# The low half of the transposed queries: from VectorE's subtraction to TensorE and a cast on ScalarE

## The chip, the core and the metric

The kernel runs on one core of one Trainium2 chip. A core has five engines, each with its own queue that it works off in order: TensorE (PE, with its weight loads shown apart as PEld), VectorE (DVE), ScalarE (ACT), GpSimd (POOL) and SyncE (SP, which here issues the DMAs). They work out of SBUF; PE writes its products to PSUM. The metric is the device time of one execution in microseconds (us), the median of several runs. Beside it stands one execution that the hardware profiler recorded; all rows of the trace come from that one.

## The reference

Two blocks are applied in turn, twice: four residual steps on an x of 2048 rows by 640 columns.

```
x = x + fourier(layernorm(x));  x = x + attention(layernorm(x))     # layer 0
x = x + fourier(layernorm(x));  x = x + attention(layernorm(x))     # layer 1

attention: 32 heads of 20;  q, k, v = x @ wqkv;  pq, pk = phi(q), phi(k)
  phi(t) = where(t > 0, t + 1, exp(t)) + 1e-6
  kv = sum over rows of pk * v;  z = sum over rows of pk
  o  = (pq @ kv) / (pq @ z + 1e-6);  result o @ wo
```

The attention is linear: keys and values are first summed over all rows, and then each row's queries are multiplied with that sum. So it needs two passes over the rows.

## The kernel before, in words

The rows lie in 16 tiles of 128. Products that need more precision than one pass of TensorE in its reduced format (fp32r) are made of **splits**: a matrix is cast to fp32r, the high half, and what is left over, the low half, is the matrix minus that cast. A product is then high x high, high x low and low x high, all summed in PSUM (`product`, L158 to L169). Of a 128 x 640 tile times a 640 x 640 matrix that makes 5 chunks x 3 x 2 halves of the columns, 30 matmuls of 320 columns. `split` (L132 to L134) makes the cast on ACT (L133) and the subtraction on DVE or POOL (L134).

A layer runs so. The Fourier block is computed on folded rows: sums and differences of mirrored rows and columns (class `Fold`), then matrices of the transform (class `Fourier`, L875 and L918). The attention's first pass (`keys_values`) takes every tile, keeps the queries phi(q) in SBUF (PQ) and sums keys and values (L237). `combine` (L345) multiplies this with the output weights, so that one 640 x 640 matrix M is left. The **second pass** (`outputs`, L448) is what the change is about. For each of 16 tiles, step n does this:

- POOL multiplies the queries of tile n+3 with the key sums (`weigh`, L417).
- PE transposes the weighted queries of tile n+1 into PSUM (`transposed`, L136 to L142), five transposes of 128 x 128.
- `weighted` (L420 to L446) makes the weights of tile n+2 on DVE: it sums each head (L430, to 32 columns), adds 1e-6 (L431), takes the reciprocal (L432) and multiplies the queries with it (L434, L440).
- PE multiplies the split queries of tile n with M: 30 matmuls on L167.
- `between()` does a piece of other work; see below.
- `split_chunks` (L144) splits the transposed queries of tile n+1 out of PSUM: ACT casts the high half, DVE subtracts. Both must be there when the product of step n+1 needs them; its first low half is used by its third pair of matmuls.
- DVE adds the product to x out of PSUM (the residual, L473), and `after` says that the tile is done.

In layer 0's second pass `between` is `Fold.tick` (L541): it already prepares layer 1's Fourier block on the first 13 tiles (PUSHED). For each finished tile ACT takes the statistics (L111, L112) and normalises (L125), POOL makes the factors (L113 to L117) and folds columns (L721 to L726), and then DVE and POOL fold rows of four tiles together (L737 to L764, L781 to L785). In layer 1's second pass there is nothing to prepare: tiles are stored, and `between` only makes a verdict on the inputs once.

The order on PE, DVE, ACT and POOL is made by the framework's own scheduler. It simulates the program in time and puts ready instructions in order by priority, first those that stand earlier in the program; AHEAD (L48) shifts the priority of named pieces, among them the splits of steps 13 and 14 ("1q13", "1q14"). Only SP's queue, and the scripts at the start of each layer, have an order written by hand. The loads of layer 1's transform matrices are gated: they wait for the residual of step 14 (GATE, L475, L813, L820).

PSUM holds four tiles of 128 x 1024. Splits come from a pool of 12 buffers (`temp`).

Of the kernel before, what the change touches and what calls it, by code (L numbers as in the profile page):

```python
# [8 lines left out]
F32 = mybir.dt.float32  # L9
# [6 lines left out]
NT = S // 128  # L16
# [34 lines left out]
class K:  # L51
    def __init__(self, tc, ctx):
        self.tc, self.nc = tc, tc.nc
        nc = self.nc
        self.n = self.layer = self.part = 0
        self.cst = ctx.enter_context(tc.tile_pool(name="cst", bufs=1))
        self.psp = ctx.enter_context(tc.tile_pool(name="ps", bufs=4, space=bass.MemoryType.PSUM))
        self.ident = self.cst.tile([128, 128], F32, name="ident")
        make_identity(nc, self.ident)
        self.ones = self.cst.tile([128, 128], F32, name="ones")  # L60
        nc.vector.memset(self.ones, 1.0)
        self.mhalf = self.cst.tile([128, 1], F32, name="mhalf")
        nc.vector.memset(self.mhalf, -0.5)

# [68 lines left out]
        self.nc.scalar.copy(hi, src)  # L133
        self.engine(pool).tensor_tensor(lo, src, hi.bitcast(F32), op=ALU.subtract)  # L134

    def transposed(self, src):  # L136
        tp = self.psum()
        for c in range(ND):
            self.nc.tensor.transpose(  # L139
                tp[:, 128 * c : 128 * c + 128], src[:, 128 * c : 128 * c + 128], self.ident  # L140
            )
        return tp  # L142

    def split_chunks(self, tp):  # L144
        hi, lo = self.temp(F32R), self.temp(F32R)
        self.split(tp[:, :D], hi, lo)
        return [[t[:, 128 * c : 128 * c + 128] for c in range(ND)] for t in (hi, lo)]


def halves(pu):  # L150
# [4 lines left out]
    return t.rearrange("p (a b) -> p a b", a=2)  # L155


def product(nc, pu, sh, sl, wh, wl, hs=range(2)):  # L158
    n, m = len(sh), sh[0].shape[1]
    for c in range(n):  # L160
        for s, w, first, last in (
            (sh[c], wh[c], c == 0, False),
            (sh[c], wl[c], False, False),
            (sl[c], wh[c], False, c == n - 1),
        ):
            for h in hs:
                nc.tensor.matmul(  # L167
                    pu[:m, 512 * h : 512 * h + HD], s, w[:, HD * h : HD * h + HD], start=first, stop=last
                )  # L169


class Attention:
# [247 lines left out]
    def weighted(self, n, t1):  # L420

        k, nc, pq = self.k, self.k.nc, self.PQ[self.order2[n]]
        heads = lambda t: t.rearrange("p (h d) -> p h d", d=DH)
        den, rden = (
            k.sm.tile([128, H], F32, tag="sm" + n, name=k.nm(n), bufs=2) for n in ("den", "rden")
        )
        nc.vector.tensor_reduce(den, heads(t1), axis=AX.X, op=ALU.add)  # L430
        nc.vector.tensor_scalar(den, den, 1e-6, None, op0=ALU.add)  # L431
# [14 lines left out]
        return t1  # L446

    def outputs(self, after, between=lambda: None):  # L448

        k, nc, X = self.k, self.k.nc, self.X  # L450
        q = self.first
        wt, t1 = self.next, self.t1
        for n, i in enumerate(self.order2):
            nxt = self.weigh(n + 3) if n + 3 < NT else None
            if n + 1 < NT:
                tp = k.transposed(wt)
            if n + 2 < NT:
                with k.ahead("weigh", n + 2):
                    wt = self.weighted(n + 2, t1)
            t1 = nxt  # L460
            pu = k.psum()
            parts = [range(2)] if n + 1 < NT else [(0,), (1,)]
            pus = [pu] + [k.psum() for _ in parts[1:]]
            for pu, hs in zip(pus, parts):
                product(nc, pu, *q, [m[0] for m in self.M], [m[1] for m in self.M], hs)
            between()
            if n + 1 < NT:
                with k.ahead("q", n):
                    q = k.split_chunks(tp)
            for pu, hs in zip(pus, parts):  # L470
                of = lambda t: t[:, hs[0] : hs[-1] + 1, :]
                with k.ahead("res", n):
                    last = nc.vector.tensor_tensor(of(h2(X[i])), of(h2(X[i])), of(halves(pu)), op=ALU.add)  # L473
# [848 lines left out]
```

## Time and profile before

| | us |
|---|---|
| median of 3 runs | 811.74 |
| lowest and highest | 809.45, 812.2 |
| the profiled execution | 813.82 |
| its span, first to last instruction | 812.1 |
| layer 0's second pass on PE | 338.7 to 425.7 |
| layer 1's second pass on PE | 733.2 to 806.2 |

PE's granted clock was 0.989 of full speed over the span. How to read the rows: a row of time has start, duration, engine, line, operation, the tiles (out<-in by the program's names), the shape and a count; the bracket at its end is idle time in front of it, and what ended it. A row of a group has the engine and line, the shape, the count, the busy time, the mean of one in ns, and the idle time in front. Tile `t` is a buffer of the common pool, `ps` one of PSUM, `w` one of the weights' pool, `den` the heads' sums. Matmuls overlap: the duration of one holds its way through the array too, so steps are read from start to start.

### The profile page before, as it was taken

The page shows a single profiled execution, that of the slowest core. Times are in us where ns is not written, and L with a number is a line of the kernel's source. Part 1 is how long each engine was busy: PE and PEld are TensorE (multiplying, and loading weights), DVE is VectorE, ACT ScalarE, POOL GpSimd, SP SyncE. Part 2 cuts the span into 40 slices and gives each one's busy share as a digit, 9 for nine tenths or more (in the row PEclk, how much of TensorE's full clock was granted, in tenths as well). Part 3 has the DMA queues.
Part 4 walks back from the last instruction along what each step waited for, and adds up shares of the span by engine and source line. Part 5 has one row for each costly group of instructions (what it writes and reads, how often), then busy time and mean ns, then how long its engine had stood idle before and what let it go on. Part 6 is the DMA issues. An engine that isn't in the chain of part 4 may idle for free. (4 is left out here: it accounts for less than half of the span.)

```text
span 812.1 us, 12968 instructions
## 1 busy us (share of the span) xinstructions
PE 747.3 (92%) x4920; PEld 711.1 (88%) x4920; DVE 622.9 (77%) x1161; ACT 344.8 (42%) x602; POOL 327.3 (40%) x356
## 2 busy tenths in 40 slices
PE   0569999999999999999888998999999999999997
PEld 0239899999999999899784888999999999989996
DVE  7798988765963575989977799877497286499982
ACT  4533544446324554365552454454633445341110
POOL 5996992111021112379885757221101111134310
PEclk9998999999999999999999999999999999999999
DMA  9122325540440422000005232454044024001121
GB/s 329 53 85 65 115 72 171 162 140 2 141 139 1 140 88 75 20 1 2 0 12 161 90 115 61 151 185 146 2 124 155 1 71 142 21 11 50 66 82 69
DMA packets 31688, 71.42 MB, mean 88 GB/s; under 512 B 3662, under 2 KB 5457, under 8 KB 31616
## 3 DMA queue, kind: packets, MB, share of 16 engines
q1 hardware_dynamic: 31584, 70.44, 27.1%
q8 instruction: 41, 0.67, 0.3%
q14 instruction: 31, 0.25, 0.1%
q0 software_dynamic: 32, 0.06, 0.1%
HBM read 64.83 MB, written 5.24 MB: 86 GB/s over the span
## 5 line engine op out<-in xcount | busy, mean ns | idle before, releaser
L167 PE MATMUL ps<-w,t 128*128 128x320 f32 x2880 | 442.5, 311 | 10.2 <-DVE t L134 5.6
L167 PEld LDWEIGHTS ps<-w,t 128*128 128x128 f32 x2880 | 424.4, 189 | 14.0 <-DVE t L134 7.6
L280 POOL TENSOR_TENSOR t<-t,s 128x640 f32<-128x640 f32 x32 | 59.0, 1845 | 218.7 <-DVE s L268 210.7
L237 PE MATMUL ps<-t,t 128*128 128x256 f32 (+1 forms) x640 | 139.9, 309 | 0.0
L265 ACT ACTIVATE t<-ps 128x640 f32<-128x640 f32 x64 | 45.2, 706 | 161.5 <-PE ps L167 151.1
L237 PEld LDWEIGHTS ps<-t,t 128*128 128x128 f32 x640 | 107.4, 188 | 0.0
L1033 DVE CUSTOM_DVE_ANT_0 junk<-ck,ck 128x688 bf16<-128x688 f32 (+4 forms) x138 | 99.8, 723 | 6.5 <-DMA ck<-in_ck 5.0
L237 PE MATMUL ps<-w,t 128*128 128x384 f32 (+1 forms) x320 | 98.5, 309 | 0.0
L417 POOL TENSOR_TENSOR t<-pq,t 128x640 f32<-128x640 f32 x32 | 56.1, 1759 | 101.3 <-ACT t L343 48.5
L134 DVE TENSOR_TENSOR t<-ps,t 128x640 fp32r<-128x640 f32 (+1 forms) x66 | 53.7, 815 | 42.4 <-ACT t L133 42.2
L133 ACT CAST t<-ps 128x640 fp32r<-128x640 f32 (+1 forms) x66 | 45.6, 692 | 65.4 <-PE ps L139 58.2
L875 PE MATMUL ps<-cw,ab 128*107 128x512 f32 (+4 forms) x108 | 43.1, 538 | 31.7 <-DVE ab L616 25.7
L875 PEld LDWEIGHTS ps<-cw,ab 128*107 128x107 f32 (+1 forms) x108 | 18.7, 184 | 50.7 <-issue 47.4
L237 PEld LDWEIGHTS ps<-w,t 128*128 128x128 f32 x320 | 60.1, 188 | 0.1
L268 DVE SCALAR_TENSOR_TENSOR pq<-t,pq 128x640 f32<-128x640 f32 x32 | 28.1, 877 | 38.6 <-ACT t L267 38.6
L918 PE MATMUL ps<-t,u 107*128 107x322 f32 (+1 forms) x306 | 51.5, 332 | 3.2 <-DVE u L900 3.2
L918 PEld LDWEIGHTS ps<-t,u 107*128 107x128 f32 (+1 forms) x306 | 50.2, 207 | 3.8 <-DVE u L900 3.7
L139 PE MATMUL ps<-ident,t 128*128 128x128 f32 x320 | 45.9, 274 | 5.3 <-DVE t L127 2.6
L267 ACT ACTIVATE t<-t 128x640 f32<-128x640 f32 x64 | 48.0, 751 | 0.0
L127 DVE TENSOR_SCALAR t<-x,kept 128x640 f32<-128x640 f32 x58 | 45.6, 787 | 1.2 <-PE ps L237 1.2
L139 PEld LDWEIGHTS ps<-ident,t 128*128 128x128 f32 x320 | 38.1, 140 | 7.8 <-DVE t L127 2.3
L134 DVE TENSOR_TENSOR t<-t,t 128x640 fp32r<-128x640 f32 x32 | 26.3, 822 | 21.8 <-ACT t L133 21.3
(178 smaller groups left out, 1017.2 us busy)
## 6 DMA issues: line engine op xcount, KB each, us to landing
ck<-in_ck SPq DMA_DIRECT2D x48, 346.0 KB
ck<-in_ck SPq DMA_DIRECT2D x48, 344.0 KB
raw<-in_wqkv SPq DMA_DIRECT2D x20, 320.0 KB
x<-in_x SPq DMA_DIRECT2D x16, 320.0 KB
out<-x SPq DMA_DIRECT2D x15, 320.0 KB
s<-in_wqkv SPq DMA_DIRECT2D x10, 320.0 KB
raw<-in_wo SPq DMA_DIRECT2D x10, 300.0 KB
ck<-in_ckr SPq DMA_DIRECT2D x6, 344.0 KB
```

The lines of the kernel that those rows point to most:

```text
L127: self.nc.vector.tensor_scalar(out, x, m, rs, op0=ALU.subtract, op1=ALU.mult)
L133: self.nc.scalar.copy(hi, src)
L134: self.engine(pool).tensor_tensor(lo, src, hi.bitcast(F32), op=ALU.subtract)
L139: self.nc.tensor.transpose(tp[:, 128 * c : 128 * c + 128], src[:, 128 * c : 128 * c + 128], self.ident)
L167: nc.tensor.matmul(pu[:m, 512 * h : 512 * h + HD], s, w[:, HD * h : HD * h + HD], start=first, stop=last)
L237: nc.tensor.matmul(self.place(G, c, part), x[:, 128 * c : 128 * c + 128], p[:, f : f + n], start=start and i == 0, stop=stop and i == 2, s ...
L267: nc.scalar.activation(e, e, AF.Exp, scale=-1.0)
L280: nc.gpsimd.tensor_tensor(pksum, pksum, pk, op=ALU.add)
L417: k.nc.gpsimd.tensor_tensor(t1, self.PQ[self.order2[n]], self.zb, op=ALU.mult)
L875: nc.tensor.matmul(pu[:m, o : o + n], e, w[:, f : f + n], start=g == 0 and i == 0, stop=g == end and not more and i == len(both) - 1,)
L918: self.k.nc.tensor.matmul(po[:, o : o + 322], s[:m, f : f + 128], w[:m, x, :], start=first, stop=last)
L1033: i = nc.vector.tensor_tensor_reduce(k.junk[:, : a.shape[1]], b, a, 1.0, 0.0, op0, op1, o)
```

## The change

In layer 0's second pass (`k.part == 1`), in steps 0 to 14, the low half of the next tile's queries is no longer made by DVE. The transposes leave the sum in PSUM open (`stop=False`). ACT casts the high half; PE multiplies it with a negated identity and adds that onto the transposes in PSUM (`take`: two matmuls, of 512 and of 128 columns), between the chunks 0 to 2 and the chunks 3 and 4 of the running product. What is then in PSUM is the low half, and ACT casts it out. So the cast of the high half stands earlier in the program, before the product, and PE waits for it after 18 of its 30 matmuls; the low half is taken after the product. In both layers the addition of 1e-6 to the heads' sums (L431) goes from DVE to ACT, with the constant as a bias tile. Layer 1's second pass keeps its split on DVE.

```diff
+        self.minus = self.cst.tile([128, 128], F32R, name="minus")
+        nc.scalar.mul(self.minus, self.ident, -1.0)
+        self.eps = self.cst.tile([128, 1], F32, name="eps")
+        nc.vector.memset(self.eps, 1e-6)
...
-    def transposed(self, src):
+    def transposed(self, src, more=False):
         tp = self.psum()
         for c in range(ND):
...
+            to, of = tp[:, 128 * c : 128 * c + 128], src[:, 128 * c : 128 * c + 128]
+            if more:
+                self.nc.tensor.matmul(
+                    to, of, self.ident, is_transpose=True, start=c % 4 == 0, stop=False, skip_group_check=True
+                )
+            else:
+                self.nc.tensor.transpose(to, of, self.ident)
         return tp
+
+    def take(self, tp, hi):
+
+        for a, b in ((0, 512), (512, D)):
+            self.nc.tensor.matmul(tp[:, a:b], self.minus, hi[:, a:b], start=False, stop=True, skip_group_check=True)
...
-def product(nc, pu, sh, sl, wh, wl, hs=range(2)):
+def product(nc, pu, sh, sl, wh, wl, hs=range(2), cs=None):
     n, m = len(sh), sh[0].shape[1]
-    for c in range(n):
+    for c in range(n) if cs is None else cs:
...
-        nc.vector.tensor_scalar(den, den, 1e-6, None, op0=ALU.add)
+        nc.scalar.activation(den, den, AF.Identity, bias=k.eps)
...
             nxt = self.weigh(n + 3) if n + 3 < NT else None
+            spare = k.part == 1 and n + 1 < NT
             if n + 1 < NT:
-                tp = k.transposed(wt)
+                tp = k.transposed(wt, spare)
+            if spare:
+                hi = k.temp(F32R)
+                with k.ahead("q", n):
+                    nc.scalar.copy(hi, tp[:, :D])
...
             for pu, hs in zip(pus, parts):
-                product(nc, pu, *q, [m[0] for m in self.M], [m[1] for m in self.M], hs)
+                for cs in ((0, 1, 2), (3, 4)):
+                    product(nc, pu, *q, [m[0] for m in self.M], [m[1] for m in self.M], hs, cs)
+                    if spare and cs[0] == 0:
+                        k.take(tp, hi)
             between()
-            if n + 1 < NT:
+            if spare:
+                lo = k.temp(F32R)
+                with k.ahead("q", n):
+                    nc.scalar.copy(lo, tp[:, :D])
+                q = k.chunks(hi, lo)
+            elif n + 1 < NT:
                 with k.ahead("q", n):
                     q = k.split_chunks(tp)
```

More of the change, by code (lines that the diff above doesn't have):

```diff
@@ L134, in split, with chunks @@
         self.engine(pool).tensor_tensor(lo, src, hi.bitcast(F32), op=ALU.subtract)
-    def transposed(self, src):
+    def transposed(self, src, more=False):
         tp = self.psum()
         for c in range(ND):
-            self.nc.tensor.transpose(
-                tp[:, 128 * c : 128 * c + 128], src[:, 128 * c : 128 * c + 128], self.ident
-            )
-        return tp
+            to, of = tp[:, 128 * c : 128 * c + 128], src[:, 128 * c : 128 * c + 128]
[5 more added lines that the diff above has]
+                self.nc.tensor.transpose(to, of, self.ident)
+        return tp
+    def take(self, tp, hi):
+        for a, b in ((0, 512), (512, D)):
+            self.nc.tensor.matmul(tp[:, a:b], self.minus, hi[:, a:b], start=False, stop=True, skip_group_check=True)
+    def chunks(self, *tiles):
+        return [[t[:, 128 * c : 128 * c + 128] for c in range(ND)] for t in tiles]
     def split_chunks(self, tp):
@@ L146, in split_chunks @@
         self.split(tp[:, :D], hi, lo)
-        return [[t[:, 128 * c : 128 * c + 128] for c in range(ND)] for t in (hi, lo)]
+        return self.chunks(hi, lo)
 def halves(pu):
```

## The prediction

> **What bounds the kernel now.** I read the page's busy line first, then busy time by stretch for the pass that is changed, then that pass on TensorE (PE) in order of time.
>
> ```profile
> PE 747.3 (92%) x4920; PEld 711.1 (88%) x4920; DVE 622.9 (77%) x1161; ACT 344.8 (42%) x602; POOL 327.3 (40%) x356
> ```
> ```profile
> 338.70:378.50 39.80, 39.74 (x279) 39.47 (x280) 36.83 (x62) 20.73 (x42) 29.11 (x41) 1.00 0.03 6
> 378.50:417.20 38.70, 32.57 (x217) 30.26 (x215) 34.94 (x50) 20.84 (x43) 35.51 (x46) 1.00 0.00 1
> 417.20:427.30 10.10, 8.48 (x56) 8.24 (x57) 7.17 (x12) 3.45 (x7) 7.66 (x13) 1.00 0.15 53
> ```
> The columns of the second fence are the stretch, its length, and busy time of PE, PE's weight loads, VectorE (DVE), ScalarE (ACT) and GpSimd (POOL). The whole is PE's: 92% busy. The changed pass runs from 338.7 to 425.7 us and has two halves. In the first PE is busy 39.74 of 39.80 us: it is the bound, and DVE's 36.83 lies beside it. In the second PE falls to 32.57 of 38.70, while POOL has 35.51 and DVE 34.94: there PE waits for the others.
>
> The matmuls of the pass in order of time (start, length, what; the bracket is idle time before, and what ended it):
>
> ```profile
> 353.79 4.65 PE L167 MATMUL ps<-w,t 128*128 128x320 f32 x30
> 358.28 0.71 PE L139 MATMUL ps<-ident,t 128*128 128x128 f32 x5
> 358.74 4.64 PE L167 MATMUL ps<-w,t 128*128 128x320 f32 x30
> ...
> 378.55 0.83 PE L167 MATMUL ps<-w,t 128*128 128x320 f32 x4
> 380.31 4.06 PE L167 MATMUL ps<-w,t 128*128 128x320 f32 x26 [0.94 <-DVE t L134]
> ...
> 389.63 0.83 PE L167 MATMUL ps<-w,t 128*128 128x320 f32 x4
> 392.62 4.09 PE L167 MATMUL ps<-w,t 128*128 128x320 f32 x26 [2.15 <-DVE t L134]
> ...
> 409.25 5.03 PE L167 MATMUL ps<-w,t 128*128 128x320 f32 x30
> ...
> 415.51 0.84 PE L167 MATMUL ps<-w,t 128*128 128x320 f32 x4 [0.68 <-ACT t L133]
> 417.25 8.48 PE L167 MATMUL ps<-w,t 128*128 128x320 f32 x56 [0.90 <-DVE t L134]
> 427.31 10.78 PE L875 MATMUL ps<-cw,ab 128*107 128x512 f32 x24 [1.57 <-DMA cw<-in_co]
> ```
> A step is five transposes and 30 matmuls, 358.74 - 353.79 = 4.95 us when dense. From step 8 on (378.55) it isn't: four matmuls, then a wait for the low half, DVE's subtraction on L134. From its start to that of step 14 (415.51) it is 37.0 us, where six dense steps take 29.7: 7.3 us lost. The last two products take 417.25 + 8.48 - 415.51 = 10.2 where dense ones take 4.49 + 4.65 = 9.1: 1.1 more. So **8.4 us of stalls** lie in the pass, and 1.57 us behind it, a wait for a DMA.
>
> Why the subtraction comes late is seen on DVE itself:
>
> ```profile
> 391.75 0.81 DVE L134 TENSOR_TENSOR t<-ps,t 128x640 fp32r<-128x640 f32 x1
> 392.49 0.80 DVE L473 TENSOR_TENSOR x<-x,ps 128x640 f32<-128x640 f32 x1
> 393.22 1.56 DVE L738 TENSOR_TENSOR ab<-ab,ab 128x640 f32<-128x640 f32 x1
> ...
> 395.43 1.73 DVE L747 TENSOR_TENSOR ab<-ab,ab 128x640 f32<-128x640 f32 x1
> 397.08 0.81 DVE L134 TENSOR_TENSOR t<-ps,t 128x640 fp32r<-128x640 f32 x1
> ```
> ```profile
> 393.32 0.74 ACT L111 ACTIVATE t<-x 128x640 f32<-128x640 f32 x1 [3.02 <-DVE x L473]
> 394.06 0.68 ACT L133 CAST t<-ps 128x640 fp32r<-128x640 f32 x1
> ...
> 414.79 0.67 ACT L133 CAST t<-ps 128x640 fp32r<-128x640 f32 x1
> ```
> In step 10 the high half was cast by 394.74; the subtraction began 2.3 us later, behind the fold (L738, L747) of the next layer. DVE's queue is in order and behind its plan. The residual L473 is late with it, and ACT's statistics (L111) wait 3.0 us for that.
>
> **What the change removes.** Fifteen subtractions leave DVE, and with them the additions of 1e-6 (L431), in both layers:
>
> ```profile
> L134 DVE TENSOR_TENSOR t<-ps,t 128x640 fp32r<-128x640 f32 x7 | 5.7, 812 | 0.3 <-ACT t L133 0.3
> L431 DVE TENSOR_SCALAR den<-den 128x32 f32<-128x32 f32 x5 | 3.2, 641 | 0.0
> ```
> These are groups of the second half alone (busy us, mean ns). Back to back a subtraction takes 0.74 us (391.75 to 392.49), so DVE gets rid of 7 x 0.74 + 3.2 = 8.4 us of the 34.94 there, 22%. Much of L431's time is waiting, 0.64 us for 32 columns; in the chain quoted below it takes 0.09. What is waiting may pass to the next instruction, so I count 7 x 0.74 + 5 x 0.09 = 5.6 us as sure and 8.4 as the most. As 7.3 + 1.1 us of stalls mostly name DVE, I expect 6.2 of the 8.4 us to go and 2.2 to stay: the stall of step 14 (1.3 us, where ACT's cast ended the first wait at 415.51) and one of ACT's new ones. Ends: all 8.4 go, or half.
>
> **What it adds on PE.** Fifteen pairs of matmuls with the negated identity, of 512 and 128 columns. The nearest rows:
>
> ```profile
> 438.63 0.39 PE L875 MATMUL ps<-cl,th 128*107 128x512 f32 x1
> 438.86 0.39 PE L875 MATMUL ps<-ch,tl 128*107 128x512 f32 x1
> ```
> ```profile
> 684.30 1.38 PE L333 MATMUL ps<-t,ones 128*128 128x128 f32 x10 [0.53 <-POOL t L280]
> 685.44 0.77 PE L237 MATMUL ps<-t,t 128*128 128x384 f32 x3
> ```
> A split product of 512 columns steps by 0.23 us. Ten products of 128 columns step by 1.14 / 10 = 0.114; five transposes of that width by (358.74 - 358.28) / 5 = 0.092. I take 0.23 + 0.09 = 0.32 us, 15 x 0.32 = **+4.9 us**; ends 4.2 (0.05 for the narrow one, a quarter of the wide) and 5.2. Nothing hides the eight pairs of steps 0 to 7, 2.6 us, where PE has no idle time; the seven others fall where it stalled.
>
> **What it adds on ACT.** Fifteen casts of 0.68 us, and the additions. Half of the ACT time is free (20.84 of 38.70 us), and 7 x 0.68 + 7 x 0.3 = 6.9 us fit. For an addition of 32 columns the trace has no row; between the 0.68 us of a cast of 640 and
>
> ```profile
> 472.10 0.16 ACT L133 CAST u<-ps 107x2 fp32r<-107x2 f32 x1 [0.32 <-DVE u L134]
> ```
> the 0.16 us of 2 columns I take 0.2, near the smaller, and 0.1 for waiting. Queued behind it on ACT are the casts, and for it waits DVE's reciprocal; but the weighting is made two steps ahead, which covers some tenths.
>
> Before layer 1's pass the chain that ends last runs through four L431 of 0.09 us on DVE:
>
> ```profile
> 714.70 0.09 DVE den L431
> ...
> 729.43 0.09 DVE den L431
> ```
> That is worth -0.3 us at most; I take -0.2. Layer 1's pass itself is PE's and stays. No DMA is added and SP's queue keeps its order. Both halves come from the same buffers as before, and the transposes hold their PSUM tile until the low half is taken, as before. The two constants at the start, some 0.5 us on ACT and DVE, lie beside loading.
>
> **The gap behind the pass.** The loads of the next transform's matrices wait for the residual of step 14:
>
> ```profile
> 423.65 0.81 DVE L473 TENSOR_TENSOR x<-x,ps 128x640 f32<-128x640 f32 x1
> 424.49 0.83 SPq L820 DMA_DIRECT2D cw<-in_co  x2
> ```
> Product 14 ends about 4.5 us before 425.73, at 421.2, so the residual began 2.4 us late, behind fold work. From its end to PE's start at 427.31 it is 2.85 us, less than one product. With DVE relieved it comes at once and the wait is covered: 1.57 us becomes 0.3, **-1.3 us**.
>
> **Sum**: +4.9 - 6.2 - 1.3 - 0.2 = **-2.8 us**. The profiled execution took 813.8 us (span 812.1), 2.1 above the median of 811.74; it becomes 811.0, and the median 808.9. That the earlier start carries through rests on
>
> ```profile
> 440.00:460.00 20.00, 17.94 (x102) 15.48 (x101) 12.74 (x17) 9.86 (x20) 10.51 (x10) 1.00 0.43 134
> ```
> where PE is busy 17.94 of 20 us behind the pass.
>
> **The rivals.**
>
> *Slower: the high half comes late on ACT.* Before, it was needed by the next product; now it is needed in the midst of this one, after 18 of 30 matmuls, 2.7 us from the start. In the second half it came later: at 394.74, 5.1 us after the product's start at 389.63. If ACT still waits for the residual ahead of the cast, PE stalls 2.4 us there. In step 13 it ended at 415.46, 6.2 us after 409.25, 3.5 too late. I take an overshoot of 2.5 us for steps 8 to 13, near the smaller. If DVE's relief takes away half, 6 x 1.25 = 7.5 us of stalls stand in place of the 8.4, and the gap stays: +4.9 - 0.9 - 0.2 = +3.8, **815.5 us**; with no relief 6 x 2.5 = 15, +11. It decides from the point where the cast ends over 2.7 us into most of those products. For it: the wait of 3.02 us above. Against: that wait was DVE's lateness, and the code now issues the cast ahead of the statistics.
>
> *No change: POOL holds the second half.* POOL is busy 35.51 of 38.70 us there, and no work is taken from it. If its work of weighing and folding sets the pace, the added matmuls fall into stalls, the pass ends where it did, and the gain is 0 to 0.5 us: **811.5 us**. For it the Trainium skill, GPSIMD Engine Reference, section "1. Specifications": POOL shares its SBUF access with DVE instructions that have two SBUF inputs or use two ports. The subtraction reads PSUM and keeps to 0.81 us between folds of 1.56 and 1.73, which agrees; so taking it away would free no time on POOL. Against: three of the four waits in the pass quoted above name DVE's L134.
>
> *The gain is given back later*: behind the pass the loads and the fold's tail bind, and the earlier start is worth less than half, some -1 us: 810.7.
>
> *The additions cost time on ACT*: if the lead of two steps doesn't cover them, each delays the weighting by 0.3 - 0.09 = 0.2 us, in the 15 steps of layer 0's pass 3 us: the sum is about 0, 811.9. The 0.64 us that DVE's own addition takes in this stage speaks against it. The Trainium skill speaks for it: ScalarE: Activation LUTs, section "Rules for kernel authors", says to add on VectorE and not on ScalarE, and its section "What ACT_TABLE_LOAD costs" gives 280 ns and 0.833 ns a column with a bias pointer, an estimate of 0.31 us for 32 columns, by which the sum would be +0.5.
>
> **Chances.** Forecast 0.56 (its own range 805.5 to 810.7), slower rival 0.28, POOL 0.08, given back 0.05, additions 0.03. Lowest: all stalls and the gap gone, 4.2 added: -5.9, 805.8, with the pair at its cheapest some tenths less. Highest: the slower rival with somewhat more than half of the overshoot. So 805.5 to 817. A measurement of this kernel can tell about 0.3%, 2.4 us, from no change. Of the forecast, whose range reaches from -6 to -1, some seven tenths lie beyond that, 0.40, and 0.01 of the gain given back: faster 0.41. The slower rival lies beyond it nearly whole: slower 0.27, same 0.32.
>
> **What would show it.** Right: in steps 0 to 7 a period of 5.27 us; from step 8 no waits over 1 us; the residual of step 14 within 1 us of its product; no DMA wait behind the pass. Wrong: waits on ACT's cast in front of the 512-column matmuls (slower rival); POOL still above 90% with the pass's end unmoved (POOL); a step of over 5.4 us where nothing waits (the pair is mis-sized).

## The result, and the profile after

| | before | after |
|---|---|---|
| median of 20 runs each, taken together on one chip, us | 812.48 | 814.76 |
| lowest and highest | 809.45, 819.75 | 812.49, 822.59 |
| the profiled execution, its span | 813.82, 812.1 | 814.74, 813.0 |
| layer 0's second pass: first product to the next block's first matmul | 338.74 to 427.31 | 338.25 to 427.70 |

After to before is 1.0050, with a 95% interval of 1.0028 to 1.0073: the change made the kernel slower, by 2.3 us in the medians, where 2.8 us of gain were forecast. Executions of every kernel here, of before too, form two groups 6 to 8 us apart, in step with two stretched instructions near 100 us that the change doesn't touch (last section); medians mix the groups, and so does the ratio, which lies near that of the means, while in the lower group alone the medians are 812.20 (17 of 20) and 814.18 (11 of 20). So beside each time below stands the length of the pass itself.

The page's busy line of after. To be read against the one in the prediction: PE has 6.6 us more, DVE 26.6 less, ACT 20.1 more, POOL the same to 0.9.

```profile
PE 753.9 (93%) x4950; PEld 715.5 (88%) x4950; DVE 596.3 (73%) x1115; ACT 364.9 (45%) x650; POOL 326.4 (40%) x356
```

Busy time by stretch, the pass cut at about the same steps as before (columns as in the prediction: stretch, length, PE, weight loads, DVE, ACT, POOL):

```profile
338.20:380.10 41.90, 41.85 (x291) 41.44 (x292) 27.70 (x45) 28.45 (x59) 29.71 (x43) 1.00 0.03 7
380.10:417.30 37.20, 32.57 (x224) 31.46 (x223) 28.53 (x40) 24.69 (x50) 33.43 (x42) 1.00 0.00 1
```

DVE has been relieved: 28.53 of 37.20 us in the second half, where it had 34.94 of 38.70. Yet PE stands still for 4.6 us there, and POOL is still at 33.43 of 37.20, 90%. The relief is real and was hardly used. PE in order of time, first a dense step, then the steps with stalls:

```profile
352.74 0.46 PE L156 MATMUL ps<-t,minus 128*128 128x512 f32 x2
353.04 0.80 PE L184 MATMUL ps<-w,t 128*128 128x320 f32 x4
353.69 0.71 PE L146 MATMUL ps<-ident,t 128*128 128x128 f32 x5
...
358.95 0.71 PE L146 MATMUL ps<-ident,t 128*128 128x128 f32 x5
...
384.32 0.45 PE L156 MATMUL ps<-t,minus 128*128 128x512 f32 x2
...
385.86 0.83 PE L184 MATMUL ps<-w,t 128*128 128x320 f32 x4
388.81 3.49 PE L184 MATMUL ps<-w,t 128*128 128x320 f32 x22 [2.12 <-ACT t L495]
...
401.78 4.08 PE L184 MATMUL ps<-w,t 128*128 128x320 f32 x26 [2.11 <-ACT t L495]
...
406.55 0.74 PE L146 MATMUL ps<-ident,t 128*128 128x128 f32 x5 [0.40 <-DVE t L457]
...
427.70 2.80 PE L905 MATMUL ps<-cw,ab 128*107 128x512 f32 x6
```

A pair steps by 353.04 - 352.74 = 0.30 us, and a dense step takes 5.26 to 5.31 us (358.95 - 353.69), 0.34 more than 4.95. The stalls have the same place in the product as before, after its fourth matmul, where the first low half is needed. Only the name in the bracket is another: ACT's cast of the low half (L495), where it was DVE's subtraction. No wait stands in front of a pair (L156): the high half was in time. The DMA wait behind the pass is gone.

What the low half waits for is seen on ACT:

```profile
384.26 0.74 ACT L115 ACTIVATE t<-x 128x640 f32<-128x640 f32 x1 [1.02 <-DVE x L503]
...
385.95 0.91 ACT L129 ACTIVATE t<-x,mv 128x640 f32<-128x640 f32 x1
386.76 0.31 ACT L448 ACTIVATE den<-den,eps 128x32 f32<-128x32 f32 x1
387.26 0.92 ACT L129 ACTIVATE t<-x,mv 128x640 f32<-128x640 f32 x1 [0.19 <-POOL mv L121]
388.09 0.67 ACT L495 CAST t<-ps 128x640 fp32r<-128x640 f32 x1
```
```profile
399.05 0.94 ACT L1134 CAST ex<-ab 1x321 fp32r<-1x321 f32 x2 [1.50 <-POOL ab L794]
400.02 0.92 ACT L129 ACTIVATE t<-x,mv 128x640 f32<-128x640 f32 x1
...
401.06 0.67 ACT L495 CAST t<-ps 128x640 fp32r<-128x640 f32 x1
```

The pair of 384.32 had put the low half into PSUM by about 384.8; ACT took it out at 388.09, behind the statistics of a tile whose residual DVE brought late (1.02 us) and behind two normalisations. The second stall is plainer: ACT stands 1.50 us for one of POOL's sums of the fold (L794), and the cast stands behind that. ACT isn't full; it waits, in order, for POOL and DVE.

### The profile page after: what moved, and what is told of

The parts are those of the page before. It is cut to its first block, busy times and chain, and to the rows that moved or that the text cites. A ratio compares the mean times of both kernels' runs of the same rounds, so it can differ in the third digit from the quotient of the medians.

```text
span 813.0 us, 13037 instructions
## 1 busy us (share of the span) xinstructions
PE 753.9 (93%) x4950; PEld 715.5 (88%) x4950; DVE 596.3 (73%) x1115; ACT 364.9 (45%) x650; POOL 326.4 (40%) x356
## 5 line engine op out<-in xcount | busy, mean ns | idle before, releaser
L434 POOL TENSOR_TENSOR t<-pq,t 128x640 f32<-128x640 f32 x32 | 54.1, 1696 | 99.6 <-ACT t L360 48.5
L138 DVE TENSOR_TENSOR t<-ps,t 128x640 fp32r<-128x640 f32 (+1 forms) x51 | 41.4, 813 | 42.5 <-ACT t L137 42.5
L948 PE MATMUL ps<-t,u 107*128 107x322 f32 (+1 forms) x306 | 49.5, 321 | 1.4 <-DVE u L930 1.4
L948 PEld LDWEIGHTS ps<-t,u 107*128 107x128 f32 (+1 forms) x306 | 47.2, 195 | 3.0 <-DVE u L930 2.2
L137 ACT CAST t<-ps 128x640 fp32r<-128x640 f32 (+1 forms) x51 | 35.4, 696 | 30.2 <-PE ps L150 28.9
L503 DVE TENSOR_TENSOR x<-x,ps 128x640 f32<-128x640 f32 (+1 forms) x34 | 26.3, 774 | 20.9 <-PE ps L184 20.9
L150 PE MATMUL ps<-ident,t 128*128 128x128 f32 x245 | 35.5, 276 | 3.3 <-DVE t L131 2.6
```

The lines of the kernel that those rows point to most:

```text
L150: self.nc.tensor.transpose(to, of, self.ident)
L434: k.nc.gpsimd.tensor_tensor(t1, self.PQ[self.order2[n]], self.zb, op=ALU.mult)
L948: self.k.nc.tensor.matmul(po[:, o : o + 322], s[:m, f : f + 128], w[:m, x, :], start=first, stop=last)
```

## The theories, and how the experiments are measured

- **The forecast's theory**: DVE's load makes the low half late. Relieve DVE, and the stalls go.
- **Rival A**: with DVE relieved, it is ACT's normalisations in front of the low cast. **Rival B**: the addition on ACT delays the weighting. **Rival C**: POOL's load alone sets the pace.
- **Theory E**, formed after the first runs: the fold of the next layer runs as one chain through the queues of POOL, DVE and ACT, each in order. What is ready stands behind links of that chain that wait for another engine. So the pass is held by the chain, whoever makes the low half.

The measure is the length from the pass's third transposes to the next block's first matmul. Dense it would be 13 steps of 4.95 us and 9.36 us for the last two products with the transposes in front of them (428.11 - 418.75, from a run below in which nothing waits there), 73.7 us; each of the 14 pairs in that stretch adds 0.34. What is over that is **lost**: stalls, and the gap for the DMA. Each length is of one profiled execution. After and e8, whose pass is the same program, agree to 0.1 us; but e1, whose time is before's, has a pass 2.3 us shorter, so differences of a few us against before's one execution need the times beside them. Times are medians, in us, with the ratio to the kernel before on the same chip. Every edit also lets the scheduler order the queues anew, so no run changes one thing alone.

| run | length | lost | time | before | ratio (95%) |
|---|---|---|---|---|---|
| before | 83.9 | 10.2 | | | |
| after | 84.6 | 6.1 | 814.76 | 812.48 | 1.0050 (1.0028, 1.0073) |
| e1: before, addition on ACT | 81.6 | 7.9 | 812.46 | 811.99 | 1.0003 (0.9963, 1.0043) |
| e2: after, addition on DVE | 85.0 | 6.6 | 814.11 | 811.99 | 1.0036 (0.9998, 1.0075) |
| e3: before, idle pairs added | 84.7 | 6.2 | 816.80 | 811.99 | 1.0038 (1.0004, 1.0073) |
| e4: after, normalisation on DVE | 88.1 | 9.6 | 822.03 | 811.99 | 1.0083 (1.0043, 1.0123) |
| e5: after, column folds on DVE | 85.7 | 7.2 | 818.29 | 816.36 | 1.0047 (1.0013, 1.0081) |
| e6: before, column folds on DVE | 85.4 | 11.7 | 818.62 | 816.36 | 1.0011 (0.9972, 1.0051) |
| e7: after, pairs in steps 7 to 14 only | 83.6 | 7.1 | 816.01 | 816.36 | 0.9986 (0.9949, 1.0023) |
| e8: after, identity negated later | 84.5 | 6.1 | 816.91 | 816.36 | 1.0024 (0.9986, 1.0062) |
| e9: before, no subtraction | 83.3 | 9.6 | 820.21 | 813.40 | 1.0036 (0.9992, 1.0081) |
| e10: before, row sums cut | 74.5 | 0.8 | 802.63 | 813.40 | 0.9888 (0.9796, 0.9980) |
| e11: after, row sums cut | 80.7 | 2.2 | 812.57 | 813.40 | 0.9974 (0.9931, 1.0018) |
| e12: after, no low cast | 83.5 | 5.0 | 818.46 | 813.40 | 1.0018 (0.9978, 1.0059) |
| e13: before, DVE's row sums cut | 80.2 | 6.5 | 810.33 | 813.04 | 0.9959 (0.9913, 1.0004) |
| e14: before, POOL's row sums cut | 78.8 | 5.1 | 807.96 | 813.04 | 0.9943 (0.9900, 0.9987) |
| e15: after, DVE's row sums cut | 82.8 | 4.3 | 819.36 | 813.04 | 1.0053 (1.0013, 1.0093) |
| e16: after, POOL's row sums cut | 81.8 | 3.3 | 816.58 | 813.04 | 1.0012 (0.9972, 1.0052) |
| e17: before, POOL's row sums on DVE | 79.3 | 5.5 | 809.54 | 812.18 | 0.9956 (0.9920, 0.9991) |
| e18: e7 with POOL's row sums on DVE | 85.4 | 9.0 | 817.70 | 812.18 | 1.0053 (1.0019, 1.0086) |

In some of these executions the lost time holds a third thing. Behind a stall, the matmuls run for a few us at a lower granted clock. In e13:

```profile
390.51 4.08 PE L167 MATMUL ps<-w,t 128*128 128x320 f32 x26 [1.46 <-DVE t L134]
...
403.58 5.61 PE L167 MATMUL ps<-w,t 128*128 128x320 f32 x26 [2.55 <-DVE t L134]
```

The same 26 matmuls take 1.5 us more the second time; the granted clock is 0.68 from 403.6 to 409.0. Such a slow stretch lies in the pass of e2, e3, e4, e6, e7, e12, e13 and e18, and two lie in that of e1; before, after, e14 and e17 have none, though before has a stall of 2.15 us and e1's second stretch follows one of 1.14. What decides it isn't shown.

## The experiments

**The parts of the change, one by one: e1, e2, e3.** e1 moves only the addition; e2 is the change without it.

```diff
 # e1, on the kernel before
-        nc.vector.tensor_scalar(den, den, 1e-6, None, op0=ALU.add)
+        nc.scalar.activation(den, den, AF.Identity, bias=k.eps)
 # e2, on the kernel after: the same line back on DVE
```

> The kernel before with only the additions of 1e-6 moved to ACT. Theory A (the low half's cast stands in ACT's queue behind statistics and norms, and that is what keeps the stalls): 811 to 812, no change against before, stalls in layer 0's second pass still 8 us and still ending in DVE's subtraction. Theory B (the hop DVE to ACT to DVE keeps DVE late): slower by 2 to 4 us, 814 to 816, with DVE's reciprocal waiting some 7 us for ACT. Theory C (GpSimd sets the pace of the second half): no change.

> The changed kernel with the additions of 1e-6 back on DVE. A: as the changed kernel, 2 to 3 us slower than before, and two waits of some 2 us in front of the low half's first use. B: 2 to 4 us faster than the changed kernel, about as before, because DVE no longer waits 7.7 us for ACT. C: as the changed kernel.

The addition costs nothing that can be measured; e2 is about as slow as the change, with 6.6 us lost. Rival B isn't supported. e3 puts fifteen pairs that add zero into the products of the kernel before, so PE has the new work while DVE keeps its subtractions:

```diff
+        nc.scalar.mul(self.nought, self.ident, 0.0)
...
+                    if k.part == 1 and n + 1 < NT and cs[0] == 0:
+                        for a, b in ((0, 512), (512, D)):
+                            nc.tensor.matmul(pu[:, a:b], k.nought, self.M[0][0][:, a:b], start=False, stop=False, skip_group_check=True)
```

> The kernel before, with the split left on ACT and DVE, and fifteen pairs of matmuls of 512 and 128 columns added to the products (a stationary matrix of zeros, so nothing is added to the result). All theories: a pair costs 0.33 us of a step where PE has no idle time. If the second half of the pass is paced by the other engines, the seven pairs there are free and the pass ends 2.6 us later; if the added time only moves everything, 5 us later. So 814.5 to 817.

This is the first run that speaks against the forecast's theory. The pass has the length of the changed kernel, 84.7 to 84.6 us, and loses as much, 6.2 to 6.1. With the pairs there, the rest of the change, the subtractions off DVE against the casts and additions put on ACT, is worth 0.1 us at most: 1.5 of what e3 loses is its slow stretch. What became of the lost time (10.2 to 6.1) came from longer steps: where PE takes 0.34 us more a step, it waits less for the others.

**Moving work off ACT or POOL onto DVE, which has room now: e4, e5, e6.**

```diff
 # e4, on the kernel after, Fold.stats: normalise the 13 tiles on DVE
-        return i, (xn, k.stats(x, xn if i in self.scalar else None))
+        return i, (xn, k.stats(x, xn if i in self.scalar else None, True))
 # e5 on after, e6 on before, Fold.fold: column sums of all tiles on DVE
-        eng = nc.gpsimd if i in self.scalar else nc.vector
+        eng = nc.vector
```

> The changed kernel with the normalisation of the 13 tiles in layer 0's second pass (12 us of ACT) on DVE instead. A: the low half's cast no longer waits behind the norms; the two waits of 2.1 us go, 4 us faster than the changed kernel, 810 to 811. B: no faster, DVE has 7 us more to do, 814 to 817. C: no faster either, 814, with GpSimd above 90% busy between 380 and 417 us.

> The changed kernel with the column sums of the fold (L721 before, 13 x 0.87 us) on DVE instead of GpSimd. Theory C (GpSimd and the fold's traffic pace the second half of the pass, whoever makes the low half): GpSimd is relieved of 11 us and DVE has room for 6, so the stalls of some 6 us in the pass shrink by half or more: 810 to 812 in runs where the first 110 us go well, against 814 for the changed kernel. Theory A (ACT's own queue): no gain, 814. If DVE is still the pace: slower, 816 or more.

> The same move in the kernel before, where DVE still makes the low halves. If DVE's load paced the pass, as the prediction had it, 6 us more on DVE cost 4 to 7 us: 816 to 819. If GpSimd paced it (C), it is no slower than before: 810 to 812.

e4 makes it worse by 3.5 us of pass. DVE got that work, so the length alone says little; but four stalls on the low cast, the longest 1.79 us, stay without the normalisations in front of it. They were not the cause by themselves, and rival A isn't supported. e5 takes POOL's busy time in the stretch from 71.88 us to 61.35 and doesn't help (85.7): POOL's load as such, rival C, isn't supported either. e6 moves the column sums of the 13 tiles from POOL to DVE, and the pass gets only 1.5 us longer.

**Which steps pay, and the instruction at the start: e7, e8.**

```diff
 # e7
-            spare = k.part == 1 and n + 1 < NT
+            spare = k.part == 1 and 7 <= n < NT - 1
 # e8: the identity is negated just ahead of the pass instead of first of all on ACT
```

> The changed kernel with the new way of making the low half only in steps 7 to 14; steps 0 to 6 split on DVE as before. All theories agree on the price of a pair where PE is the bound: 7 x 0.33 = 2.3 us less, 811.5 to 812. If the added time in the early steps is taken out of later stalls anyway (C), the gain is under 1 us.

> The changed kernel with its order of instructions untouched but for one: the negated identity is made on ACT ahead of the second pass and not as ACT's first instruction. Theory D (that instruction shifts the first 100 us, where DVE's normalisation is starved by GpSimd in some executions, 7 us longer, 20 per cent of them before and nearly half with the instruction): executions of 819 us and more fall to one in five, the others stay at 814. Without D: as the changed kernel, nearly half of them long.

e7 keeps the pairs only where PE waited, and saves the price of the early ones: level with before. Nothing is gained even where PE has the time. e8 changes nothing.

**The gain taken alone: e9, e12.** e9 is the kernel before without the subtraction; the high half stands in for the low one. No pair and no cast is paid for. e12 is the changed kernel with the pairs but without the low half's cast.

```diff
 # e9, on the kernel before (layer 0's second pass)
-                    q = k.split_chunks(tp)
+                    q = k.split_chunks(tp, k.part == 1)
...
+        if alone:
+            self.nc.scalar.copy(hi, tp[:, :D])
+            lo = hi
 # e12, on the kernel after
-                    nc.scalar.copy(lo, tp[:, :D])
-                q = k.chunks(hi, lo)
+                q = k.chunks(hi, hi)
```

> The kernel before, but in steps 0 to 14 of layer 0's second pass the subtraction of the low half is left out and the high half is used in its place (the products come out wrong in their low terms). No pair is added, and ACT gets no second cast. This is what the forecast counted as the gain, taken alone. Forecast's theory (DVE's load makes the low half late; 7 x 0.74 us off DVE take 6.2 of the 8.4 us of stalls): the pass from its third transposes to the Fourier block's first matmul falls from 83.9 to 75 to 77 us, and the time by 6 to 8 us, to 804 to 806 with 812 before. Theory E (the second half is held by the next layer's fold, whose chain runs over DVE, POOL and ACT, whoever makes the low half): the pass stays at 81 to 84 us and the time within 2.5 us of before; stalls beside the groups of four (steps 8 to 13) stay, and name the high half's cast on ACT.

> The changed kernel with the pairs on TensorE, but the low half isn't cast out of PSUM; the high half is used in its place (the products come out wrong in their low terms). DVE has no subtraction and ACT no second cast. Theory E: the pass stays at 82.5 to 85 us (84.6 in the changed kernel) and the time within 2 us of the changed kernel's 814. If the low cast's place in ACT's queue is the cause of the stalls that stayed: the pass falls to 79 to 81 us, and the time by 4 to 6 us, to 808 to 810.

e9 settles the failed step. The very load that the forecast reckoned with is gone, free of charge. Busy time in the measured stretch, of before and then of e9 (DVE is the third busy time, POOL the fifth):

```profile
343.40:427.31 83.91, 76.15 (x520) 73.56 (x521) 74.25 (x114) 44.87 (x89) 70.71 (x97) 1.00 0.02 7
```
```profile
350.90:434.15 83.25, 74.88 (x521) 73.62 (x520) 62.34 (x99) 44.61 (x89) 71.67 (x97) 1.00 0.02 7
```

DVE is busy 11.9 us less, and the pass is 83.3 us long, 0.6 less than before. Without the gap for the DMA the lost time did shrink, from 8.6 to 5.6 us, about half of what was forecast; but that gap grew from 1.57 to 3.94 us and took most of it back. The time shows no gain: the lower group of e9 takes 812.4 to 814.0 us, that of before beside it 809.2 to 814.7 (seven of e9's ten lie in the upper group). Where the gain went is seen behind the last steps of e9, first DVE, then ACT, SP's queue and PE:

```profile
428.97 1.58 DVE L777 TENSOR_TENSOR tl<-ab,th 128x640 fp32r<-128x640 f32 x1 [3.11 <-ACT th L772]
430.47 0.80 DVE L477 TENSOR_TENSOR x<-x,ps 128x640 f32<-128x640 f32 x1
```
```profile
426.58 0.92 ACT L125 ACTIVATE t<-x,mv 128x640 f32<-128x640 f32 x1 [1.88 <-POOL mv L117]
...
428.22 0.71 ACT L772 CAST th<-ab 128x640 fp32r<-128x640 f32 x1
```
```profile
431.30 0.83 SPq L824 DMA_DIRECT2D cw<-in_co  x2
```
```profile
421.17 9.04 PE L171 MATMUL ps<-w,t 128*128 128x320 f32 x60
434.15 6.32 PE L879 MATMUL ps<-cw,ab 128*107 128x512 f32 x11 [3.94 <-DMA cw<-in_co]
```

Product 14 ended in the midst of those 60 matmuls, at about 425.7. Its residual (L477, 430.47) was ready to run from then on, and DVE was idle for 3.11 us: but the next in DVE's queue was L777, which waited for ACT's cast L772, which stood behind a normalisation, which waited 1.88 us for POOL's factor. The loads, gated by that residual, went out at 431.30, and PE waited 3.94 us for them. An idle engine with a ready instruction, behind one that isn't ready: DVE's load has no part in this wait. e12 says the same for ACT: without the low cast the pass is only 1.1 us shorter, and the stalls name the high half's cast. (Six of its ten executions lie in the upper group; the others take 811.7 to 814.2 us.)

**The fold's row sums cut, on both engines: e10, e11.** The sums and differences of four tiles work on 8 of 640 columns in that part of the program, so most of the fold over rows is left out, in the pass and in the script behind it.

```diff
+        w = slice(0, 8 if k.part == 1 else D)
-        nc.vector.tensor_tensor(a, a, d, op=ALU.add)
+        nc.vector.tensor_tensor(a[:, w], a[:, w], d[:, w], op=ALU.add)
         # and so b + c, a - b, a + b and both lines of even()
```

> The kernel before, but in layer 0's second pass the fold's sums over rows of four tiles (additions and subtractions of whole 128 x 640 tiles on DVE and POOL) work on 8 of 640 columns only: most of the fold over rows is left out, the instructions stay. Theory E: the stalls of steps 8 to 13 go nearly whole, the pass falls from 83.9 us to 74.5 to 76.5, and the time by 6 us or more. A theory in which the two-deep chain of weights (POOL's weighing, DVE's sums, ACT) holds the second half: stalls of 4 us or more stay and the pass is 79 us or more.

> The changed kernel with the same sums over rows of four tiles cut to 8 of 640 columns (most of the fold over rows left out). Theory E: the stalls go here too and the pass becomes the dense one with fifteen pairs, 78.6 to 80.5 us; against the same cut in the kernel before it is then longer by the full price of the pairs, 13 x 0.34 = 4.4 us in that stretch. If ACT's second cast is late by itself (ACT's queue, not the fold): stalls of 2 us or more that name the low cast stay, and the pass is 82 us or more.

Busy time in that stretch, of e10 and then of e11:

```profile
341.70:416.16 74.46, 73.97 (x522) 73.62 (x521) 63.96 (x115) 44.66 (x89) 59.10 (x97) 1.00 0.03 10
```
```profile
349.10:429.77 80.67, 79.64 (x550) 77.83 (x549) 46.45 (x84) 55.88 (x115) 58.51 (x98) 1.00 0.03 9
```

With the row sums cut the stalls are gone: PE is busy 73.97 of 74.46 us, subtractions and all, with DVE at 63.96. In the changed kernel DVE has 46.45, and the pass is 6.2 us longer, 4.8 of it the pairs. (The expectation counted 13 pairs; there are 14.) e11 ends 0.2 us above its range, with one stall of 0.99 us on the low cast.

**DVE's or POOL's share: e13 to e16.** The same cut, only on DVE's ten whole sums or only on POOL's four.

```diff
 # e14 and e16 (e13 and e15: the others)
-        self.k.engine(EVENS[g]).tensor_tensor(d, a, b, op=ALU.add)
+        w = slice(0, 8 if self.k.part == 1 else D)
+        self.k.engine(EVENS[g]).tensor_tensor(d[:, w], a[:, w], b[:, w], op=ALU.add)
         # and b + c where PAIRS[g] gives it to POOL
```

> The kernel before with only DVE's share of the fold's sums over rows cut to 8 of 640 columns in layer 0's second pass (ten whole-tile instructions of about 1.2 us; that part of the fold is left out). POOL's four whole sums stay. Load of DVE as the cause: nearly all of the gain of e10 is here, the pass from its third transposes to the Fourier block's first matmul is 74.5 to 77 us (83.9 before). Chain over the queues: about two thirds of the gain by size, 76 to 79 us, and a stall that follows one of POOL's whole sums stays.

> The kernel before with only POOL's four whole sums of the fold over rows cut to 8 of 640 columns in that pass (about 6 us of POOL; that part of the fold is left out), DVE's ten whole. Load of DVE as the cause: the pass stays within 1.5 us of before, 82.4 to 85 us. Chain over the queues: 3 us or more of the 10 us of stalls and gap go, the pass is 77 to 81 us.

> The changed kernel with DVE's share of the sums cut as in e13. Load of DVE as the cause: like e11, 80 to 81.5 us (84.6 in the changed kernel). Chain: 81 to 83 us, with a stall of 1 us or more on ACT's low cast left.

> The changed kernel with POOL's four whole sums cut as in e14. Load of DVE as the cause: within 1.5 us of the changed kernel's 84.6. Chain: 80.5 to 82.5 us, most of what e11 gained, since with the subtraction gone DVE has room and POOL's place in the chain weighs more.

Busy time in the stretch, of e13 and then of e14:

```profile
343.10:423.29 80.19, 76.08 (x520) 75.16 (x521) 67.59 (x115) 44.90 (x89) 63.87 (x97) 0.98 0.03 9
```
```profile
341.40:420.22 78.82, 75.30 (x520) 73.66 (x521) 70.20 (x113) 44.85 (x89) 64.02 (x97) 1.00 0.03 10
```

Cutting ten sums on DVE saves 3.7 us of pass, or 5.2 without e13's slow stretch; cutting four on POOL saves 5.1. In the changed kernel it is 1.9 and 2.8. DVE's load doesn't order these runs: with 74.25 us in before, it is 62.34 in e9, 67.59 in e13 and 70.20 in e14, and the pass is shorter by 0.6, 3.7 and 5.1 us.

Neither cut is a clean one, though. POOL's busy time falls from 70.71 to 63.87 us in e13, and DVE's from 74.25 to 70.20 in e14, where none of that engine's own work was cut: the instructions of one get shorter when the other has less to do. How much of the gain is this, and how much the place of the sums in the queues, no run here separates. The expectation for e13 under theory E, 76 to 79, was too low by 1.2 us, less than the 1.5 of the slow stretch.

**Made use of: e17, e18.** The row sums that POOL makes in the pass go to DVE, in the kernel before (e17) and in e7 (e18).

```diff
-        self.k.engine(EVENS[g]).tensor_tensor(d, a, b, op=ALU.add)
+        self.k.engine(EVENS[g] and (self.k.part != 1 or g == 3)).tensor_tensor(d, a, b, op=ALU.add)
-        k.engine(PAIRS[g]).tensor_tensor(b, b, c, op=ALU.add)
+        k.engine(k.part != 1 and PAIRS[g]).tensor_tensor(b, b, c, op=ALU.add)
```

> The kernel before, POOL's four whole sums of the fold over rows in layer 0's second pass made by DVE (nothing left out). DVE gets four instructions of 0.8 to 1.2 us, POOL loses four of 1.57. Chain over the queues, POOL's place in it the costliest: the pass gets shorter, 80.5 to 83 us against 83.9, the time -1 to -2 us. DVE's load as the cause: longer by 2 to 4 us.

> The changed kernel with the pairs and the second cast only in steps 7 to 14 (the steps before keep the subtraction on DVE), and POOL's four whole sums made by DVE (nothing left out). If TensorE's pair frees room on DVE that the sums can use, this is where the change could pay: pass 80 to 82 us, time 809 to 811, below before's 811.6. If DVE's room doesn't count: pass 83 us or more, time within 1 us of before or above.

e17, over the second half, then its residual of step 14 on DVE, then PE:

```profile
383.50:418.80 35.30, 30.80 (x213) 29.73 (x212) 33.46 (x51) 20.39 (x41) 30.46 (x42) 1.00 0.00 1
```
```profile
423.89 0.82 DVE L473 TENSOR_TENSOR x<-x,ps 128x640 f32<-128x640 f32 x1 [0.41 <-PE ps L167]
```
```profile
418.75 0.71 PE L139 MATMUL ps<-ident,t 128*128 128x128 f32 x5
419.21 9.06 PE L167 MATMUL ps<-w,t 128*128 128x320 f32 x60
428.11 4.45 PE L875 MATMUL ps<-cw,ab 128*107 128x512 f32 x10
```

DVE, the engine that the change meant to relieve, gets four instructions more, is at 33.46 of 35.30 us (95%), and the pass is 4.7 us shorter. Over the whole measured stretch DVE's busy time is 72.6 us, less than before's 74.25 in spite of the four: here too it gains from what POOL no longer does. The residual of step 14 waits for nothing but its product, and the gap is gone. The time is 809.54 against 812.18, ratio 0.9956 (0.9920 to 0.9991): a version faster than both kernels, and by more than the 1 to 2 us expected. e18 went the second of its two ways, DVE's room doesn't count. With pairs and the second cast it loses 9.0 us, 1.5 of them in a slow stretch; ACT shows why:

```profile
416.51 0.92 ACT L129 ACTIVATE t<-x,mv 128x640 f32<-128x640 f32 x1 [2.20 <-POOL mv L121]
417.34 0.67 ACT L495 CAST t<-ps 128x640 fp32r<-128x640 f32 x1
```

The low cast stands behind a normalisation that waits 2.20 us for POOL's factor; PE's stall there is 2.41 us. On DVE (e17) the low half had no such neighbour. The same moved sums that help with the low half on DVE don't with the low half on ACT.

## Why the prediction was wrong

**The failed step** is "I expect 6.2 of the 8.4 us to go". In the profiled pair of executions the pass went from 88.57 us (427.31 - 338.74) to 89.45 (427.70 - 338.25), +0.9. The pairs cost 15 x 0.34 = 5.1 and the gap gave 1.6 back, so 2.6 us of stalls went. By e3 the longer step alone does as much, and by e9 the relief alone takes 3.0 us of stalls, of which 2.4 come back in the gap: 0.6 us. The stalls "mostly name DVE", and DVE was busy 34.94 of 38.70 us; from both I concluded that DVE's load made it late. But the releaser in a bracket is only the last link. Behind it can stand a queue in order whose head waits for another engine. Rows of before show it:

```profile
411.84 0.92 ACT L125 ACTIVATE t<-x,mv 128x640 f32<-128x640 f32 x1 [3.07 <-POOL mv L117]
```
```profile
415.00 1.46 DVE L739 TENSOR_TENSOR ab<-ab,ab 128x640 f32<-128x640 f32 x1 [2.37 <-POOL ab L726]
416.39 0.81 DVE L134 TENSOR_TENSOR t<-ps,t 128x640 fp32r<-128x640 f32 x1
```

The stall of 0.90 us in front of 417.25 names DVE's subtraction, the one of 416.39. Its high half had been there since 415.46. But DVE had stood idle for 2.37 us until POOL's column fold (L726) let L739 start, and the subtraction came behind that. ACT had waited 3.07 us for POOL's factor ahead of the cast of 414.79. Not every stall is like this: ahead of the subtraction of step 10 (397.08) DVE did work without a break.

What the runs show in its place is that the fold's row sums make the stalls (e10, where 0.8 us is left of the 10.2), and the four on POOL more than their number (e14, e17). That this goes by the order of the queues is read from the rows; no run isolates it from the instructions that lengthen each other.

Of the signs named for being right, three came true: a period of 5.26 to 5.31 us, the residual of step 14 about 0.3 us behind its product, no DMA wait. The one that carried the gain, no wait over 1 us from step 8 on, did not: 2.12 and 2.11 us.

The other terms:

- **The pair on PE**: 0.34 us a step for a forecast 0.32, 5.1 for +4.9 (15 x 0.32 is 4.8). Right.
- **The share of DVE**: 8.4 of 34.94 us is 24%, not 22%; it went down by 6.4, to 28.53.
- **The gap**: -1.6 for -1.3. Right in size, by luck. The loads go out at 424.57, no earlier than the 424.49 of before. The wait is covered because the changed pass ends later: product 14 at about 423.4, 2.2 us later than the 421.2 of before, with the residual at 423.73. And in before the residual of 423.65 wasn't held by load: DVE stood idle for 2.01 us in front of the instruction ahead of it, for a cast on ACT.

```profile
424.57 0.83 SPq L850 DMA_DIRECT2D cw<-in_co  x2
```
```profile
422.40 1.33 DVE L773 TENSOR_TENSOR tl<-ab,th 128x640 fp32r<-128x640 f32 x1 [2.01 <-ACT th L768]
```

- **The addition on ACT**: 0.31 us (386.76) for 0.2. The estimate from the Trainium skill, ScalarE: Activation LUTs, "What ACT_TABLE_LOAD costs", was 0.31; this trace agrees. Its price is hidden (e1, e2), though in the changed pass DVE stands 7.7 us in all for it, where e1 has 0.8.
- **Layer 1**, -0.2 forecast, is +0.5: from 427.70 to the end of the span it is 385.3 us, from 427.31 it was 384.8. Without the additions DVE's order changes in front of the second pass, the verdict's reduction (L1087) comes behind a head sum, and PE waits for it:

```profile
733.03 0.17 PE L1089 MATMUL ps<-ident,cktop 8*1 8x8 f32 x1 [1.54 <-DVE cktop L1087]
733.13 0.76 PE L150 MATMUL ps<-ident,t 128*128 128x128 f32 x5
```

  In before, PE waited 0.96 us there, for the weighting (L440), so not the whole wait is new: the transposes start 305.43 us behind 427.70, where they started 305.10 behind 427.31, and 0.3 of the 0.5 us is this. e1, which moves only the additions, shows the same wait of 1.53 us. The price for an order that shifts was not in the sum.
- **The sum**: +0.9 in the pass and +0.5 behind it, with a pass that begins 0.5 us earlier. So the profiled pair differs by +0.9 us, the medians by 2.3. The rest I can't show in a trace. Before's profiled execution lies 1.3 to 2.1 us above its medians, and e1, the same pass but for the additions, loses 7.9 us there, 3.1 of them in slow stretches, and not 10.2: the stalls that I counted in one execution may be more than the usual one has. That stays open.

**The rivals.** *The high half late on ACT* (0.28) had the side right and the place wrong: no pair waited for it; ACT's lateness struck the low half. *POOL holds the second half* (0.08) comes nearest: POOL stayed at 90%, and the added matmuls fell into stalls. Its load as such isn't what holds (e5); its row sums are part of it (e14, e17). I set 0.08 on it because three of four brackets named DVE; they named who came last. The sentence from the Trainium skill there, GPSIMD Engine Reference, "1. Specifications", that DVE and POOL share SBUF access, agrees with e9. Without the subtraction, which reads PSUM, POOL's weighing in the second half is no faster; the groups of before and of e9:

```profile
L417 POOL TENSOR_TENSOR t<-pq,t 128x640 f32<-128x640 f32 x5 | 8.6, 1728 | 0.1
```
```profile
L421 POOL TENSOR_TENSOR t<-pq,t 128x640 f32<-128x640 f32 x5 | 9.1, 1821 | 0.2
```

That each engine's instructions get longer when the other has more to do is seen in e13 and e14; how much of the loss that is, no run here took apart.

## What to carry to other kernels

A stall that names an engine doesn't say that this engine has too much work: look at whether the late instruction was ready while its engine was idle or worked on something that came late, and follow that to the queue where the waiting starts. Before relieving an engine, leave the work out altogether in one run and look at the ceiling of the gain; here it was 0.6 us of pass, where 6.2 had been counted. Four sums moved from POOL to the engine that seemed overloaded gave more than fifteen instructions taken off it.

## What the hardware showed unexpectedly

In the executions of the upper group two DVE instructions of layer 0's Fourier block last longer: the normalisation on L127, 5.84 us instead of 1.05 to 1.90, and an addition just ahead of it (L943), 3.76 to 3.89 instead of 0.55 to 0.75. Before, then e17, whose profiled execution is of the upper group:

```profile
101.97 0.75 DVE L943 TENSOR_TENSOR x<-x,t 128x321 f32<-128x321 f32 x1
103.44 1.05 DVE L127 TENSOR_SCALAR t<-x,kept 128x640 f32<-128x640 f32 x1
```
```profile
99.11 3.89 DVE L943 TENSOR_TENSOR x<-x,t 128x321 f32<-128x321 f32 x1
103.73 5.84 DVE L127 TENSOR_SCALAR t<-x,kept 128x640 f32<-128x640 f32 x1
```
```profile
109.71 1.30 PE L139 MATMUL ps<-ident,t 128*128 128x128 f32 x5 [6.79 <-DVE t L127]
```

PE's transposes wait 6.79 us for the normalisation, about the distance between the two groups. Meanwhile POOL, in e17:

```profile
103.86 0.85 POOL L950 TENSOR_TENSOR x<-x,t 128x321 f32<-128x321 f32 x1
...
107.79 0.85 POOL L950 TENSOR_TENSOR x<-x,t 128x321 f32<-128x321 f32 x1
108.59 0.62 POOL L253 MEMSET t<- 128x640 f32 x1
```

From 103.86 on it runs five additions and subtractions back to back, and the DVE instruction ends (109.57) just behind the memset that follows them. Of the 20 profiled executions of this study ten show the long values, of both instructions, and ten the short; there is nothing between. That POOL's instructions hold DVE off is read from the rows, not tried. What decides which way an execution goes wasn't found either: e8, which takes the changed kernel's new ACT instruction away from the start, has as many in the upper group (6 of 12) as others.
